# Seven block products for eight in the second gated stage of a fused attention and MLP kernel

## The chip, the cores and the metric

One core of a Trainium2 chip runs the whole program. The metric is the device time of one execution in microseconds (us). The engines are TensorE (PE, with its weight loads shown apart as PEld), VectorE (DVE), ScalarE (ACT), GpSimd (POOL) and SyncE (SP), which here issues nearly all DMAs.

## What is computed

Three parts follow each other on 3072 tokens of 384 features. The last one is the part that the change touches.

```
x1 = leaky_mlp(gated_linear_attention(q, k, v, alpha))   # first part and stage 1: 384 -> 2048 -> 384
a  = x1 @ w1                                             # 384 -> 1024
b  = x1 @ w2                                             # 384 -> 1024
out = ((a * b) @ w3) @ w_out                             # 1024 -> 1024 -> 384
```

All of it is in 32 bits. The kernel folds `w3 @ w_out` into one 1024 x 384 matrix, called w34, so that the last line is one product.

## The kernel before, in words

A product of two 32-bit operands is made of three matmuls: each operand is split into a rounded high part (by an ACT copy) and the rest (by a DVE subtraction), and high by high, high by low and low by high are summed in one PSUM bank (`three`, L418, `mm3`, L413, whose matmuls all carry L416; `split`, L152 to L154). A matmul has 128 rows of contraction, 128 outputs and 512 tokens (384 columns for w34). The tokens are six tiles T of 512.

The attention and stage 1 run interleaved for T = 0 to 5: `G1` makes a block f of the 16 of the hidden layer (nine matmuls, then ACT, DVE, ACT, DVE at L428, L430, L435, L436), and `G2` two blocks later adds its output product (L444 to L447). While the last tile, T = 5, runs in stage 1, the attention is over, and the kernel loads and splits the weights of stage 2 beside it: `load_wo2`, `load_w3`, `load_x1(0)` and `convert_w12` (L532 to L567). The split w1 and w2 blocks take the places of the stage 1 weights `r_in[j]` that have been used: 16 blocks, of which four are started in T = 5 (`TAIL`) and twelve in the next step.

Then w34 is made (L595 to L606): eight times 24 matmuls of 384 columns, called tile `w` in the profile, its results split into `r_out[0..7]` (L600, L601).

Stage 2 (L662 to L679) goes over 6 tiles and 8 blocks j of 128 hidden features. `product` makes the banks of a and b for (T, j), nine matmuls each (three blocks of 128 features times three), tile `ab`; ACT copies a out, DVE multiplies b by it (L624), ACT and DVE split the product (L73, L627; tile `cs`). `project` then makes the output product of the block before, nine matmuls into three banks (tile `acc<-cs`), and after the last block copies the banks out and writes them (L635 to L637). So the matmuls of one block's output product stand behind the next block's input products. `load_x1(T + 1)` reads and splits a tile of x1 (L555 to L557), one tile ahead. `extremes` reads the attention's alpha back in eight pieces and takes its smallest and largest values (L643 to L647); `verdict` (L649 to L660) sets a flag from them that selects a slow repetition after the end if alpha is out of its range, which it is not here.

The order on SP is that of the program. On the other engines instructions are put in order when the kernel is built, by priority and by a model of their times, except where `keep_in_program_order` fixes the order. PSUM has eight banks of 512 columns: `pacc` has six, under the names acc0, acc1 and acc2 with _0 or _1, and `pab` has two. A bank, or an SBUF buffer of a pool, is written again when what read it has ended. `later(k, fn)` runs fn k calls of `tick()` later.

Of the kernel before, what the change touches and what calls it, by code (L numbers as in the profile page):

```python
# [9 lines left out]
F32 = mybir.dt.float32  # L10
# [6 lines left out]
AX = mybir.AxisListType  # L17
# [25 lines left out]
BEHIND = 400  # L43
BLK = 2 * DM
NSP = NJ * (3 * DM + 1024)
TAIL = 4
ALPHA_MIN, ALPHA_MAX = 0.78, 1.28
P_FLOOR = 2.0 ** -60

# [15 lines left out]
def fused_kernel(ctx, tc, qk, al, vv, wf, ws, m_alpha, ident, maskn, out):  # L65
# [90 lines left out]
    def flat(ap):  # L156
        return ap if len(ap.shape) == 2 else ap.rearrange("p a b -> p (a b)")
# [296 lines left out]
    with tc.manual_schedule(engines={mybir.EngineType.SP}):  # L454
# [66 lines left out]
        for g in range(NG + LAG):  # L521
            T, f = seq[g] if g < NG else (NTA, 0)
            if (T, f) == (NTA - 1, 2):
                attn.close()
                late = ExitStack()
                wl = late.enter_context(tc.tile_pool(name="wl", bufs=1))
                w34 = ExitStack()
                wsp = w34.enter_context(tc.tile_pool(name="ws", bufs=1))
                wo2_s = wsp.tile([128, 2, NJ, DM], F32R, name="wo2_s")
                w3_s = []  # L530

                def load_wo2(j):  # L532
                    t = wsp.tile([128, DM], F32, tag="y34", name="wo2", bufs=3)
                    sp.dma_start(out=t, in_=wo2_d[:, j])
                    later(2, lambda: split(wo2_s[:, 0, j], wo2_s[:, 1, j], t, dve))

                def load_w3(i):
                    y = wsp.tile([128, NJ, 128], F32, tag="y34", name="w3y", bufs=3)
                    sp.dma_start(out=flat(y), in_=w3_d[:, i * 1024:(i + 1) * 1024])
                    t = wsp.tile([128, 2, NJ, 128], F32R, tag="w3", name="w3", bufs=2)  # L540
                    for k in range(0, NJ, 4):
                        q = slice(k, k + 4)
                        if i < 2:
                            later(3 + k // 4, lambda q=q: split(t[:, 0, q], t[:, 1, q], y[:, q], dve))
                        else:
                            split(t[:, 0, q], t[:, 1, q], y[:, q], dve)
# [6 lines left out]
                def load_x1(T):  # L553
                    y = wl.tile([128, KD, TA], F32, tag="x1y", name="x1y")
                    sp.dma_start(out=y, in_=x1_d[T])  # L555
                    new_x(T)
                    split(xt[T][:, 0], xt[T][:, 1], y, dve)  # L557

                later(2 * SETTLE, lambda: load_x1(0))
                left = list(range(2 * NJ))  # L560

                def convert_w12():
                    j = left.pop(0)
                    t = r_in[j]
# [30 lines left out]
        for i in range(NJ):  # L595
            t = w3_s[i]
            ps = bank([128, DM], "w34", 0)
            mm3(ps, [m for k in range(NJ) for m in three((t[:, 0, k], t[:, 1, k]), (wo2_s[:, 0, k], wo2_s[:, 1, k]))],
                True, True)
            copy(r_out[i][:, 0], ps)  # L600
            dve.tensor_tensor(out=r_out[i][:, 1], in0=ps, in1=f32(r_out[i][:, 0]), op=ALU.subtract)  # L601
            if i + 2 < NJ:
                load_w3(i + 2)
            while len(left) > (NJ - 1 - i) * (2 * NJ - TAIL) // NJ:
                convert_w12()
            tick()  # L606
        while due:
            tick()
        w34.close()
        load_x1(1)  # L610
        wx = late.enter_context(tc.tile_pool(name="wx", bufs=1))

        def product(j, x):
            ps = []
            for i in range(2):
                w = r_in[2 * j + i]
                p = pab.tile([128, TA], F32, tag="h", name="ab")
                mm3(p, [m for k in range(KD) for m in three((w[:, 0, k], w[:, 1, k]), (x[:, 0, k], x[:, 1, k]))],
                    True, True)
                ps.append(p)  # L620
            a = gp.tile([128, TA], F32, tag="m", name="a", bufs=1)
            copy(a, ps[0])
            c = gp.tile([128, TA], F32, tag="g", name="c")
            dve.tensor_tensor(out=c, in0=ps[1], in1=a, op=ALU.mult)  # L624
            s = gp.tile([128, 2, TA], F32R, tag="gs", name="cs", bufs=3)
# [4 lines left out]
        def project(j, s, accs, dst, op):  # L630
            for m in range(KD):
                c = slice(m * 128, (m + 1) * 128)
                mm3(accs[m], three((r_out[j][:, 0, c], r_out[j][:, 1, c]), (s[:, 0], s[:, 1])), j == 0, j == NJ - 1)
                if j == NJ - 1:
                    o = op.tile([128, TA], F32, tag="x1", name="o", bufs=KD)  # L635
                    copy(o, accs[m])
                    sp.dma_start(out=dst[m * 128:(m + 1) * 128], in_=o)  # L637

        NPART = 2 * B
        ext = wx.tile([128, 2, NPART], F32, name="ext")  # L640
        alv = al.rearrange("b (u c) p a t -> (b u) p c (a t)", u=2)

        def extremes(i):  # L643
            t = wx.tile([128, NC_B // 2, NP * CH], F32, tag="alx", name="alx")
            sp.dma_start(out=t, in_=alv[i])
            later(6, lambda: [dve.tensor_reduce(out=ext[:, a, i:i + 1], in_=t, op=op, axis=AX.XY)
                              for a, op in enumerate((ALU.min, ALU.max))])  # L647

        def verdict():  # L649
# [7 lines left out]
            ps = pab.tile([1, 1], F32, tag="h", name="cnt")  # L657
            for a in range(2):
                pe.matmul(ps, bad[:, a:a + 1], one, start=a == 0, stop=a == 1)
            dve.tensor_copy(flag, ps)  # L660

        prev = None  # L662
        for q in range(NTA * NJ):
            T, j = divmod(q, NJ)
            if j == 0:
                if 1 <= T < NTA - 1:
                    load_x1(T + 1)
                accs = None
            if q % 4 == 2 and q // 4 < NPART:
                extremes(q // 4)  # L670
            if q == 4 * NPART + 10:
                verdict()
            s = product(j, xt[T])
            if prev:
                project(*prev)
            accs = accumulators((T + 1) % 2) if j == 0 else accs
            prev = (j, s, accs, out[:, T * TA:(T + 1) * TA], wx)
            tick()
        project(*prev)  # L679
        assert not due  # L680
    late.close()

# [1 line left out]
    with tc.If(bad > 0):  # L684
# [85 lines left out]
                sp.dma_start(out=x1_d[bass.ds(T, 1)].rearrange("b p k t -> p (b k) t"), in_=x)  # L770

        with tc.tile_pool(name="fx", bufs=2) as fx:
            with tc.For_i(0, NTA, 1) as T:
                y = fx.tile([128, KD, TA], F32, name="x1")
                sp.dma_start(out=y, in_=x1_d[bass.ds(T, 1)].rearrange("b p k t -> p (b k) t"))
# [1 line left out]
                split(e[:, 0], e[:, 1], y, dve)  # L777
                accs = accumulators(0)
                for j in range(NJ):
                    project(j, product(j, e), accs, out[:, bass.ds(T * TA, TA)], gp)  # L780


# [49 lines left out]
```

## Time and profile before

| | |
|---|---|
| Median of 3 runs | 845.78 us (845.17 to 845.91) |
| Profiled execution, first to last instruction | 850.3 us (the page gives this span alone and no time around it) |
| Mean granted TensorE clock | 0.992 of full speed |
| PE busy | 827.5 us, 97% |
| DVE busy | 458.1 us, 54% |
| ACT busy | 355.3 us, 42% |
| HBM read and written | 75.63 MB and 18.35 MB |

The profiled execution is 4.5 us longer than the median. A busy PE is not by itself a PE at its peak, since matmuls overlap; the spacing of matmuls in the chain of waits tells more.

### The profile page before, as it was taken

The page shows a single profiled execution, that of the slowest core. Times are in us where ns is not written, and L with a number is a line of the kernel's source. Part 1 is how long each engine was busy: PE and PEld are TensorE (multiplying, and loading weights), DVE is VectorE, ACT ScalarE, POOL GpSimd, SP SyncE. Part 2 cuts the span into 40 slices and gives each one's busy share as a digit, 9 for nine tenths or more (in the row PEclk, how much of TensorE's full clock was granted, in tenths as well). Part 3 has the DMA queues.
Part 4 walks back from the last instruction along what each step waited for, and adds up shares of the span by engine and source line. Part 5 has one row for each costly group of instructions (what it writes and reads, how often), then busy time and mean ns, then how long its engine had stood idle before and what let it go on. Part 6 is the DMA issues. An engine that isn't in the chain of part 4 may idle for free.

```text
span 850.3 us, 12693 instructions
## 1 busy us (share of the span) xinstructions
PE 827.5 (97%) x5158; PEld 676.9 (80%) x5158; DVE 458.1 (54%) x640; ACT 355.3 (42%) x562; POOL 14.5 (2%) x56
## 2 busy tenths in 40 slices
PE   7889899999999999999999999999999999999996
PEld 4567788888888788878888889988888888888885
DVE  6899966765776477656435634552433435222221
ACT  3567655444554455554435534422223232222222
POOL 1010000000000000000000000000000000000000
PEclk9999999999999999999999999999999999999999
DMA  8557555321654466536003306420302203010101
GB/s 314 180 206 216 181 206 180 99 87 52 217 185 169 149 217 215 166 135 209 33 19 112 124 1 221 142 84 1 127 21 75 75 19 131 1 38 0 38 1 41
DMA packets 49106, 99.60 MB, mean 117 GB/s; under 512 B 4880, under 2 KB 25488, under 8 KB 49040
## 3 DMA queue, kind: packets, MB, share of 16 engines
q1 hardware_dynamic: 48800, 98.62, 34.3%
q8 instruction: 42, 0.69, 0.3%
q14 instruction: 24, 0.20, 0.1%
q10 hardware_dynamic: 240, 0.10, 0.0%
HBM read 75.63 MB, written 18.35 MB: 111 GB/s over the span
## 4 chain that ended last, share of the span: by engine, by line
PE 80%; DVE 7%; DMA 4%; ACT 3%; issue 2%; SPq 1%; DVEq 0%; ACTq 0%
PE ab L416 23%; PE h L416 18%; PE acc L416 12%; PE acc L444 6%; PE acc L445 6%; PE acc L447 6%; PE w L416 4%; DMA al<-in_al_dram 3%; PE uy L247 2%; DMA qk<-in_qk_dram 1%; PE scp L247 1%; DVE y L149 1%; DVE g L430 1%; DVE al L221 1%; DVE sc L282 1%
## 5 line engine op out<-in xcount | busy, mean ns | idle before, releaser
L416 PE MATMUL h<-x,w 128*128 128x512 f32 x864 | 214.7, 393 | 3.9 <-DVE g L430 2.3
L416 PE MATMUL ab<-x,w 128*128 128x512 f32 x864 | 203.7, 389 | 0.0
L416 PEld LDWEIGHTS h<-x,w 128*128 128x128 f32 x864 | 161.4, 188 | 40.3 <-DVE g L430 3.3
L416 PEld LDWEIGHTS ab<-x,w 128*128 128x128 f32 x864 | 162.1, 188 | 33.6
L444 PE MATMUL acc<-gs,w 128*128 128x512 f32 x288 | 115.2, 400 | 0.0
L624 DVE TENSOR_TENSOR c<-ab,a 128x512 f32<-128x512 f32 x48 | 33.1, 690 | 148.3 <-PE ab L416 148.2
L445 PE MATMUL acc<-gs,w 128*128 128x512 f32 x288 | 112.7, 391 | 0.0
L430 DVE SCALAR_TENSOR_TENSOR g<-h,salpha,u 128x512 f32<-128x512 f32 x96 | 71.7, 747 | 72.2 <-ACT u L428 72.2
L416 PE MATMUL acc<-cs,w 128*128 128x512 f32 x432 | 105.8, 389 | 0.0
L428 ACT ACTIVATE u<-h,sgn 128x512 f32<-128x512 f32 x96 | 65.4, 681 | 85.9 <-PE h L416 85.8
L435 ACT ACTIVATE gs<-g,sgn 128x512 fp32r<-128x512 f32 x96 | 69.3, 722 | 72.1 <-DVE g L430 72.0
L436 DVE SCALAR_TENSOR_TENSOR gs<-g,sgn,gs 128x512 fp32r<-128x512 f32 x96 | 71.8, 748 | 42.6 <-ACT gs L435 41.6
L416 PEld LDWEIGHTS acc<-cs,w 128*128 128x128 f32 x432 | 81.0, 188 | 17.2 <-DVE cs L627 0.4
L447 PE MATMUL acc<-gs,w 128*128 128x512 f32 x288 | 80.9, 389 | 0.0
L73 ACT ACTIVATE a<-ab 128x512 f32<-128x512 f32 x48 | 28.7, 597 | 113.5 <-PE ab L416 113.5
L73 ACT ACTIVATE cs<-c 128x512 fp32r<-128x512 f32 x48 | 30.2, 630 | 89.9 <-DVE c L624 89.9
L444 PEld LDWEIGHTS acc<-gs,w 128*128 128x128 f32 x288 | 54.4, 189 | 12.8 <-issue 1.0
L447 PEld LDWEIGHTS acc<-gs,w 128*128 128x128 f32 x288 | 54.1, 188 | 11.5
L445 PEld LDWEIGHTS acc<-gs,w 128*128 128x128 f32 x288 | 54.4, 189 | 10.6
L627 DVE TENSOR_TENSOR cs<-c,cs 128x512 fp32r<-128x512 f32 x48 | 33.2, 691 | 30.8 <-ACT cs L73 30.8
L142 ACT ACTIVATE top<-raw 128x768 f16<-128x768 bf16 (+1 forms) x39 | 41.7, 1069 | 18.0 <-DVE y L149 9.4
L221 DVE TENSOR_TENSOR_SCAN al<-al,scan 128x516 f32<-128x516 f32 x24 | 29.4, 1227 | 24.6 <-DMA al<-in_al_dram 24.6
(73 smaller groups left out, 682.0 us busy)
## 6 DMA issues: line engine op xcount, KB each, us to landing
raw<-in_ws_dram SPq DMA_DIRECT2D x22, 767.8 KB, 5.3
qk<-in_qk_dram SPq DMA_DIRECT2D x24, 512.0 KB, 4.8
raw<-in_wf_dram SPq DMA_DIRECT2D x16, 767.8 KB, 6.0
ws_d<-y SPq DMA_DIRECT2D x22, 384.0 KB, 2.6
al<-in_al_dram SPq DMA_DIRECT2D x24, 256.0 KB, 4.1
v<-in_vv_dram SPq DMA_DIRECT2D x24, 256.0 KB, 4.8
alx<-in_al_dram SPq DMA_DIRECT2D x8, 768.0 KB, 4.5
x_d<-x1e SPq DMA_DIRECT2D x18, 256.0 KB, 4.2
```

The source lines that it names most:

```text
L73: act.activation(out=out, in_=in_, func=AF.Copy)
L142: ins = act.activation(out=z[:, :n].bitcast(F16).rearrange("p (n c) -> p n c", c=2)[:, :, 1], in_=t.bitcast(BF16)[:, :, 2], func=AF.Copy)
L221: scan = dve.tensor_tensor_scan(out=flatP, data0=flatP, data1=scan1.rearrange("p a t -> p (a t)"), initial=0.0, op0=ALU.mult, op1=ALU.max)
L416: pe.matmul(ps, w, x, start=first and i == 0, stop=last and i == n - 1)
L428: both = [act.activation(out=u, in_=ps, func=AF.Identity, scale=sg)]
L430: both += [dve.scalar_tensor_tensor(out=gt, in0=ps, scalar=sa, in1=u, op0=ALU.mult, op1=ALU.max)]
L435: act.activation(out=s[:, 0], in_=gt, func=AF.Identity, scale=sg)
L436: dve.scalar_tensor_tensor(out=s[:, 1], in0=gt, scalar=sg, in1=f32(s[:, 0]), op0=ALU.mult, op1=ALU.subtract)
L444: pe.matmul(acc[T][m], r_out[f][:, 0, c], s[:, 0], start=f == 0, stop=False)
L445: pe.matmul(acc[T][m], r_out[f][:, 1, c], s[:, 0], start=False, stop=False)
L447: pe.matmul(acc[T][m], r_out[f][:, 0, c], s[:, 1], start=False, stop=f == NF - 1)
L627: dve.tensor_tensor(out=s[:, 1], in0=c, in1=f32(s[:, 0]), op=ALU.subtract)
```

## The change

Stage 2 takes two tiles, T and T + 1, at a time. For a block j the input products form a matrix of two rows (w1's and w2's block j) by two columns (the two tiles), summed over three blocks of 128 features, which is twelve block products. Over the first two feature blocks the eight products are replaced by seven (Strassen's method in Winograd's form); the third feature block keeps its four. That is 11 block products for 12, so 33 matmuls for 36 in each `unit` (pair p, block j). The weights' combinations s1 to s4 are made once in `convert_w12`, the tokens' t1 to t4 once for each pair in `x_blocks`. Of the products that share a bank, a later one is added onto what ACT or DVE has read out between (`first=False`).

The order of all matmuls of stage 2 is fixed as written (`pinned`). The output product of the pair's first tile runs two blocks behind (`behind`, `LAG` = 2); that of the second tile (`cs2`, eight buffers) runs behind the pair, 24 matmuls for each of three banks (`fin`). The last group of a unit (`rest`, called `tail`) is put into the next unit. w34 goes to `r_out[8..15]`, since `r_out[0..7]` hold weight combinations. Alpha's extremes are taken in 24 pieces for eight, and the verdict moves to the last pair's end. The diff, cut to its core:

```diff
+    w34 = r_out[NJ:]
...
                 def load_w3(i):
-                    y = wsp.tile([128, NJ, 128], F32, tag="y34", name="w3y", bufs=3)
+                    for k in range(0, NJ, 4):
+                        y = wsp.tile([128, 4, 128], F32, tag="y34", name="w3y", bufs=4)
...
                 def convert_w12():
                     j = left.pop(0)
-                    y = wsp.tile([128, DM], F32, tag="w12", name="w12", bufs=3)
-                    sp.dma_start(out=y, in_=w12_d[:, j])
-                    split(flat(t[:, 0]), flat(t[:, 1]), y, dve)
+                    y = wsp.tile([128, 2, KD, 128], F32, tag="w12", name="w12", bufs=2)
+                    sp.dma_start(out=y, in_=w12_d[:, 2 * j:2 * j + 2].rearrange("p i (k c) -> p i k c", k=KD))
+                    (a11, a12, a13), (a21, a22, _) = ([y[:, i, k] for k in range(KD)] for i in range(2))
+                    split(r_in[2 * j][:, 0], r_in[2 * j][:, 1], y[:, 0], dve)
+                    for to, x0, x1, op in ((a13, a11, a21, ALU.subtract), (a21, a21, a22, ALU.add),
+                                           (a11, a21, a11, ALU.subtract), (a12, a12, a11, ALU.subtract)):
+                        dve.tensor_tensor(out=to, in0=x0, in1=x1, op=op)
+                    split(r_in[2 * j + 1][:, 0], r_in[2 * j + 1][:, 1], y[:, 1], dve)
+                    split(r_out[j][:, 0], r_out[j][:, 1], flat(y[:, 0]), dve)
+                def x_blocks(p, part):
...
+                    if part == 0:
+                        b = [read(2 * p, 0), read(2 * p + 1, 0), read(2 * p, 1)]
...
+                        keep("b11", b[0])
+                        minus(b[0], b[1], b[0])
+                        keep("t1", b[0])
+                        keep("b21", b[2])
+                        xb["raw"] = b + [read(2 * p + 1, 1)]
+                        return
...
+                    minus(t1, b22, t1)
+                    keep("t2", t1)
+                    keep("b22", b22)
+                    minus(b21, b21, t1)
+                    minus(b12, b22, b12)
+                    b31, b32 = read(2 * p, 2), read(2 * p + 1, 2)
+                    keep("b31", b31)
+                    keep("b32", b32)
+                    keep("t3", b12)
+                    keep("t4", b21)
...
-            if T == NTA - 1 and f >= NF - TAIL:
+            if T == NTA - 1 and f % 2 == 1 and f > 1:
                 later(2, convert_w12)
...
+        def unit(j, tail, behind):
...
+            u, y = (pacc.tile([128, TA], F32, tag=f"acc{i}_{j % 2}", name="uy"[i]) for i in range(2))
+            go(u, ("a11", "b11"))
+            copy(c1, u)
+            go(y, ("a12", "b21"), ("a13", "b31"))
+            dve.tensor_tensor(out=c1, in0=y, in1=c1, op=ALU.add)
+            tail()
+            z = pacc.tile([128, TA], F32, tag="acc2_0", name="z")
+            go(z, ("s1", "t1"))
+            copy(p5, z)
+            behind(0)
+            behind(1)
+            go(u, ("s2", "t2"), first=False)
+            copy(c2, u)
+            go(z, ("s4", "b22"), ("a13", "b32"), first=False)
+            dve.tensor_tensor(out=c2, in0=z, in1=c2, op=ALU.add)
+            go(y, ("a23", "b32"))
+            behind(2)
+            go(u, ("s3", "t3"), first=False)
+            dve.tensor_tensor(out=b2, in0=u, in1=p5, op=ALU.add)
+            dve.tensor_tensor(out=b2, in0=y, in1=b2, op=ALU.add)
+            dve.tensor_tensor(out=c2, in0=c2, in1=b2, op=ALU.mult)
+            second = split_c(c2, "cs2", NJ)
+            def rest():
+                go(u, ("a22", "t4"), ("a23", "b31"), first=False)
+                dve.tensor_tensor(out=c1, in0=u, in1=c1, op=ALU.mult)
+                first.append(split_c(c1, "cs1", 3))
...
+            for j in range(NJ):
+                extremes(q)
+                behind = (lambda m, j=j: add_out(j - LAG, m, cs1[j - LAG][0], accs[m])) if j >= LAG else nothing
+                tail, a, b = unit(j, tail, behind)
...
+            for j in range(NJ - LAG, NJ):
+                if j == NJ - 1:
+                    tail()
+                for m in range(KD):
+                    add_out(j, m, cs1[j][0], accs[m]) if j < NJ - 1 else None
+            if p + 1 < NTA // 2:
+                x_blocks(p + 1, 0)
+            fin = [pacc.tile([128, TA], F32, tag=f"acc{m}_0", name="o2") for m in range(2)]
+            for m in range(KD):
+                if m == 1:
+                    for i in range(KD):
+                        add_out(NJ - 1, i, cs1[NJ - 1][0], accs[i])
+                        emit(T, i, accs[i])
+                    if p + 1 < NTA // 2:
+                        x_blocks(p + 1, 1)
+                    else:
+                        verdict()
+                if m == 2:
+                    fin.append(pacc.tile([128, TA], F32, tag="acc2_1", name="o2"))
+                for j in range(NJ):
+                    add_out(j, m, cs2[j], fin[m])
+                emit(T + 1, m, fin[m])
```

`keep` is a `split` of one block, `read` one DMA of a 128 x 512 block of x1 into one of four buffers, and `emit` a copy and a DMA of one output bank through three buffers. `x_blocks(0, 0)` is set off in T = 5 and `x_blocks(0, 1)` in the first step of w34. The slow repetition behind the end is adapted to the new places of the weights and does not run.

## Rows read from the trace of the kernel before

**Rows 1.** The page, busy time of each engine over the span.
```profile
PE 827.5 (97%) x5158; PEld 676.9 (80%) x5158; DVE 458.1 (54%) x640; ACT 355.3 (42%) x562; POOL 14.5 (2%) x56
```

**Rows 2.** Busy time by stretch: T = 5 of stage 1, w34, stage 2.
```profile
core 0: us, PE busy (x) PEld busy (x) DVE busy (x) ACT busy (x) POOL busy (x), PEclk, DMA share, GB/s
451.20:515.73 64.53, 64.53 (x286) 53.46 (x285) 32.67 (x48) 31.73 (x51) 0.00 (x0) 1.00 0.23 78
515.73:549.03 33.30, 33.30 (x193) 33.30 (x193) 18.65 (x32) 17.83 (x35) 0.00 (x0) 1.00 0.63 213
549.03:843.54 294.51, 294.50 (x1301) 242.88 (x1299) 100.56 (x123) 73.49 (x118) 0.00 (x0) 1.00 0.13 46
```

**Rows 3.** The chain in order of time through stage 2: start us, us, what.
```profile
549.03 8.20 PE ab L416 x36
557.24 2.04 PE acc L416 x9
559.27 4.08 PE ab L416 x18
...
839.15 4.39 PE acc L416 x18
```

**Rows 4.** Groups by line and shape from 515.7 us on: busy us, mean ns.
```profile
L416 PE MATMUL ab<-x,w 128*128 128x512 f32 x864 | 203.7, 389 | 0.0
L416 PE MATMUL acc<-cs,w 128*128 128x512 f32 x432 | 105.8, 389 | 0.0
L627 DVE TENSOR_TENSOR cs<-c,cs 128x512 fp32r<-128x512 f32 x48 | 33.2, 691 | 30.8 <-ACT cs L73 30.8
L73 ACT ACTIVATE cs<-c 128x512 fp32r<-128x512 f32 x48 | 30.2, 630 | 89.9 <-DVE c L624 89.9
L73 ACT ACTIVATE a<-ab 128x512 f32<-128x512 f32 x48 | 28.7, 597 | 113.5 <-PE ab L416 113.5
L646 DVE TENSOR_REDUCE ext<-alx 128x1 f32<-128x1536 f32 x16 | 27.5, 1747 | 9.1 <-DMA alx<-in_al_dram 9.1
L154 DVE TENSOR_TENSOR x<-x1y,x 128x1536 fp32r<-128x1536 f32 x5 | 8.8, 1758 | 3.7 <-ACT x L73 3.7
L154 DVE TENSOR_TENSOR w<-w,w 128x384 fp32r<-128x384 f32 x12 | 6.4, 555 | 4.7 <-ACT w L73 4.7
```

**Rows 5.** Timeline where w34 ends and stage 2 begins.
```profile
549.07 0.49 ACT L73 ACTIVATE w<-w 128x384 fp32r<-128x384 f32 x1 [3.67 <-PE w L416]
549.59 0.56 DVE L601 TENSOR_TENSOR w<-w,w 128x384 fp32r<-128x384 f32 x1 [0.43 <-ACT w L73]
551.15 0.60 ACT L73 ACTIVATE a<-ab 128x512 f32<-128x512 f32 x1 [1.59 <-PE ab L416]
```

**Rows 6.** Timeline of the end.
```profile
840.65 0.69 DVE L627 TENSOR_TENSOR cs<-c,cs 128x512 fp32r<-128x512 f32 x1 [0.70 <-ACT cs L73]
841.40 1.70 PEld L416 LDWEIGHTS acc<-cs,w 128*128 128x128 f32 x8 [0.40 <-DVE cs L627]
842.80 2.32 SPq L637 DMA_DIRECT2D out_dram<-o  x3
```

**Rows 7.** Timeline of DVE in T = 5, one late `g` and the next.
```profile
473.97 1.76 DVE L154 TENSOR_TENSOR x<-x1y,x 128x1536 fp32r<-128x1536 f32 x1 [0.80 <-ACT x L73]
475.65 0.74 DVE L430 SCALAR_TENSOR_TENSOR g<-h,salpha,u 128x512 f32<-128x512 f32 x1
...
478.17 0.74 DVE L430 SCALAR_TENSOR_TENSOR g<-h,salpha,u 128x512 f32<-128x512 f32 x1
```

**Rows 8.** DMA issues: KB each, median us from issue to landing.
```profile
al<-in_al_dram SPq DMA_DIRECT2D x24, 256.0 KB, 4.1
...
x1y<-x_d SPq DMA_DIRECT2D x6, 768.0 KB, 5.9
out_dram<-o SPq DMA_DIRECT2D x18, 256.0 KB, 2.1
```

**Rows 9.** Timeline of PE at two waits in earlier stages.
```profile
293.62 0.74 PE L247 MATMUL uy<-v,kT 128*64 128x64 f32 x16 [1.98 <-ACT x1e L73]
...
375.20 0.69 PE L247 MATMUL uy<-v,kT 128*64 128x64 f32 x16 [0.95 <-ACT x1e L73]
```

**Rows 10.** Stretches around these two waits; the column behind POOL is the granted clock.
```profile
292.00:294.00 2.00, 0.38 (x12) 0.39 (x14) 0.40 (x1) 1.97 (x5) 0.00 (x0) 1.00 0.00 0
294.00:296.00 2.00, 2.00 (x29) 1.67 (x24) 0.00 (x0) 0.54 (x2) 0.00 (x0) 0.53 0.03 8
296.00:298.00 2.00, 2.00 (x50) 2.00 (x48) 0.78 (x2) 0.82 (x3) 0.00 (x0) 0.62 0.00 0
...
375.00:377.00 2.00, 1.80 (x44) 1.63 (x48) 0.00 (x0) 1.12 (x3) 0.00 (x0) 1.00 0.00 0
```

More of the change, by code (lines that the diff above doesn't have):

```diff
@@ L45 @@
 NSP = NJ * (3 * DM + 1024)
-TAIL = 4
 ALPHA_MIN, ALPHA_MAX = 0.78, 1.28
@@ L525, in fused_kernel @@
                 late = ExitStack()
-                wl = late.enter_context(tc.tile_pool(name="wl", bufs=1))
-                w34 = ExitStack()
-                wsp = w34.enter_context(tc.tile_pool(name="ws", bufs=1))
+                wl = late.enter_context(tc.tile_pool(name="wl", bufs=4))
+                w34p = ExitStack()
+                wsp = w34p.enter_context(tc.tile_pool(name="ws", bufs=1))
                 wo2_s = wsp.tile([128, 2, NJ, DM], F32R, name="wo2_s")
@@ L552, in fused_kernel @@
                     later(NJ + 1 + 2 * i, lambda i=i: load_w3(i))
[L553 to L560, printed above, removed]
+                left = list(range(NJ))
                 def convert_w12():
                     j = left.pop(0)
[L564 to L567 removed]
+                    y = wsp.tile([128, 2, KD, 128], F32, tag="w12", name="w12", bufs=2)
[7 more added lines that the diff above has]
+                    split(r_out[j][:, 0], r_out[j][:, 1], flat(y[:, 0]), dve)
@@ new lines, in x_blocks, with read, keep, minus @@
+                def x_blocks(p, part):
+                    def read(T, k):
+                        y = wl.tile([128, TA], F32, tag="x1y", name="x1y")
+                        sp.dma_start(out=y, in_=x1_d[T][:, k])
+                        return y
+                    def keep(name, y):
+                        t = xb[name]
+                        split(t[:, 0], t[:, 1], y, dve)
+                    def minus(to, x0, x1):
+                        dve.tensor_tensor(out=to, in0=x0, in1=x1, op=ALU.subtract)
+                    if part == 0:
+                        b = [read(2 * p, 0), read(2 * p + 1, 0), read(2 * p, 1)]
+                        t = xp.tile([128, 2, KD, TA], F32R, tag="x", name="xb0")
+                        for i, name in enumerate(("b11", "b21", "t1")):
+                            xb[name] = t[:, :, i]
+                        keep("b11", b[0])
[4 more added lines that the diff above has]
+                        return
+                    t1, b12, b21, b22 = xb.pop("raw")
+                    t = xp.tile([128, 2, KD, TA], F32R, tag="x", name="xb1")
+                    for i, name in enumerate(("t2", "b22", "b32")):
+                        xb[name] = t[:, :, i]
+                    for name in ("b31", "t3", "t4"):
+                        xb[name] = gp.tile([128, 2, TA], F32R, tag="gs", name="xb2", bufs=3)
+                    minus(t1, b22, t1)
[8 more added lines that the diff above has]
+                    keep("t4", b21)
@@ L569, in fused_kernel @@
+                xb = {}
+                later(2 * SETTLE, lambda: x_blocks(0, 0))
             if g in spans:
@@ L599, in fused_kernel @@
                 True, True)
-            copy(r_out[i][:, 0], ps)
-            dve.tensor_tensor(out=r_out[i][:, 1], in0=ps, in1=f32(r_out[i][:, 0]), op=ALU.subtract)
+            copy(w34[i][:, 0], ps)
+            dve.tensor_tensor(out=w34[i][:, 1], in0=ps, in1=f32(w34[i][:, 0]), op=ALU.subtract)
             if i + 2 < NJ:
                 load_w3(i + 2)
-            while len(left) > (NJ - 1 - i) * (2 * NJ - TAIL) // NJ:
+            if left:
                 convert_w12()
+            if i == 0:
+                x_blocks(0, 1)
             tick()
@@ L608, in fused_kernel, with pinned, duo, blocks_of @@
             tick()
-        w34.close()
-        load_x1(1)
+        w34p.close()
         wx = late.enter_context(tc.tile_pool(name="wx", bufs=1))
[L613 to L625, printed above, removed]
+        def pinned(ps, pairs, first=True, last=True):
+            n = len(pairs)
+            for i, (w, x) in enumerate(pairs):
+                tc.keep_in_program_order(pe.matmul(ps, w, x, start=first and i == 0, stop=last and i == n - 1,
+                                                   skip_group_check=True))
+        def duo(t, k):
+            return t[:, 0, k], t[:, 1, k]
+        def blocks_of(j):
+            r3 = r_out[j].rearrange("p h (k c) -> p h k c", k=KD)
+            names = ("a11", "a12", "a13", "s1", "a22", "a23", "s2", "s4", "s3")
+            tiles = [r_in[2 * j]] * KD + [r_in[2 * j + 1]] * KD + [r3] * KD
+            return {n: duo(t, i % KD) for i, (n, t) in enumerate(zip(names, tiles))}
+        def split_c(c, tag, bufs):
+            s = wx.tile([128, 2, TA], F32R, tag=tag, name=tag, bufs=bufs)
             copy(s[:, 0], c)
@@ L628, in product, with add_out, emit @@
             return s
[L630 to L639, printed above, removed]
+        def add_out(j, m, s, ps):
+            c = slice(m * 128, (m + 1) * 128)
+            pinned(ps, three((w34[j][:, 0, c], w34[j][:, 1, c]), (s[:, 0], s[:, 1])), j == 0, j == NJ - 1)
+        def emit(T, m, ps):
+            o = gp.tile([128, TA], F32, tag="x1", name="o", bufs=KD)
+            copy(o, ps)
+            sp.dma_start(out=out[m * 128:(m + 1) * 128, T * TA:(T + 1) * TA], in_=o)
+        NPART = NSTEP
         ext = wx.tile([128, 2, NPART], F32, name="ext")
-        alv = al.rearrange("b (u c) p a t -> (b u) p c (a t)", u=2)
         def extremes(i):
-            t = wx.tile([128, NC_B // 2, NP * CH], F32, tag="alx", name="alx")
-            sp.dma_start(out=t, in_=alv[i])
-            later(6, lambda: [dve.tensor_reduce(out=ext[:, a, i:i + 1], in_=t, op=op, axis=AX.XY)
+            t = wx.tile([128, NP, CH], F32, tag="alx", name="alx")
+            sp.dma_start(out=t, in_=al[i // NC_B, i % NC_B])
+            later(1, lambda: [dve.tensor_reduce(out=ext[:, a, i:i + 1], in_=t, op=op, axis=AX.XY)
                               for a, op in enumerate((ALU.min, ALU.max))])
@@ L656, in verdict @@
                 dve.tensor_scalar(out=bad[:, a:a + 1], in0=m[:, a:a + 1], scalar1=lim, scalar2=None, op0=cmp)
-            ps = pab.tile([1, 1], F32, tag="h", name="cnt")
+            ps = pacc.tile([1, 1], F32, tag="acc1_1", name="cnt")
             for a in range(2):
-                pe.matmul(ps, bad[:, a:a + 1], one, start=a == 0, stop=a == 1)
+                tc.keep_in_program_order(pe.matmul(ps, bad[:, a:a + 1], one, start=a == 0, stop=a == 1))
             dve.tensor_copy(flag, ps)
-        prev = None
@@ L663, in fused_kernel @@
[L663 to L677, printed above, removed]
-            tick()
@@ new lines, in fused_kernel @@
+        nothing = lambda *_: None
+        for p in range(NTA // 2):
+            T = 2 * p
+            tail = nothing
+            cs1, cs2 = [], []
+            accs = [pacc.tile([128, TA], F32, tag="acc2_1", name="o0")]
+            accs += [pab.tile([128, TA], F32, tag="h", name="o1") for _ in range(2)]
+            for j in range(NJ):
+                q = p * NJ + j
+                extremes(q)
+                behind = (lambda m, j=j: add_out(j - LAG, m, cs1[j - LAG][0], accs[m])) if j >= LAG else nothing
+                tail, a, b = unit(j, tail, behind)
+                cs1.append(a)
+                cs2.append(b)
+                tick()
+            for j in range(NJ - LAG, NJ):
[5 more added lines that the diff above has]
+                x_blocks(p + 1, 0)
+            tick()
+            fin = [pacc.tile([128, TA], F32, tag=f"acc{m}_0", name="o2") for m in range(2)]
[13 more added lines that the diff above has]
+                emit(T + 1, m, fin[m])
+            tick()
@@ L772, in fused_kernel, with product, project @@
         with tc.tile_pool(name="fx", bufs=2) as fx:
+            for j in range(NJ):
+                t = r_in[2 * j + 1]
+                y = fx.tile([128, DM], F32, name="w2y")
+                sp.dma_start(out=y, in_=w12_d[:, 2 * j + 1])
+                split(flat(t[:, 0]), flat(t[:, 1]), y, dve)
+            def product(j, x):
+                ps = []
+                for i in range(2):
+                    w = r_in[2 * j + i]
+                    p = pab.tile([128, TA], F32, tag="h", name="ab")
+                    mm3(p, [m for k in range(KD) for m in three((w[:, 0, k], w[:, 1, k]), (x[:, 0, k], x[:, 1, k]))],
+                        True, True)
+                    ps.append(p)
+                a = gp.tile([128, TA], F32, tag="m", name="a", bufs=1)
+                copy(a, ps[0])
+                c = gp.tile([128, TA], F32, tag="g", name="c")
+                dve.tensor_tensor(out=c, in0=ps[1], in1=a, op=ALU.mult)
+                s = gp.tile([128, 2, TA], F32R, tag="gs", name="cs", bufs=3)
+                copy(s[:, 0], c)
+                dve.tensor_tensor(out=s[:, 1], in0=c, in1=f32(s[:, 0]), op=ALU.subtract)
+                return s
+            def project(j, s, accs, dst):
+                for m in range(KD):
+                    c = slice(m * 128, (m + 1) * 128)
+                    mm3(accs[m], three((w34[j][:, 0, c], w34[j][:, 1, c]), (s[:, 0], s[:, 1])), j == 0, j == NJ - 1)
+                    if j == NJ - 1:
+                        o = gp.tile([128, TA], F32, tag="x1", name="o", bufs=KD)
+                        copy(o, accs[m])
+                        sp.dma_start(out=dst[m * 128:(m + 1) * 128], in_=o)
             with tc.For_i(0, NTA, 1) as T:
@@ L779, in fused_kernel @@
                 for j in range(NJ):
-                    project(j, product(j, e), accs, out[:, bass.ds(T * TA, TA)], gp)
+                    project(j, product(j, e), accs, out[:, bass.ds(T * TA, TA)])
 def kernel(**inputs):
```

19 lines of the change are left out of this document (14 added, 5 removed).

## The prediction

> **What bounds the kernel now.** I read the page first: PE is busy for 97% of the span, DVE for half, ACT for less [rows 1]. An average over stages says little, so the stretches come next: in T = 5 of stage 1, in w34 and in stage 2 PE is busy without a gap, at full granted clock, while DVE is busy 51%, 56% and 34% of the time [rows 2]. Since a busy PE need not be at its pace, the chain comes third. In stage 2 it is PE alone: 36 matmuls in 8.20 us, 9 in 2.04, 18 in 4.08, and so on to the end [rows 3]. Each is 0.2267 us per matmul (8.16 / 36, 2.04 / 9), whether nine follow each other into one bank (ab) or three banks take three each (acc). The 864 + 432 = 1296 matmuls [rows 4] would take 293.8 us at that pace; the stretch is 294.5 [rows 2]. So 0.7 us of stage 2 is waiting, and only fewer matmuls can shorten it.
>
> **The sum** is taken as differences in the profiled execution (span 850.3 us, the only time its page gives) and applied to the median of the runs, 845.78; stage 2 runs at one steady pace there, so I carry the differences over unscaled. 0.2%, or 1.7 us, is about what a measurement of this kernel can tell from no change.
>
> *Removed.* In each of 3 x 8 units 33 input matmuls stand for 36. That is 72 matmuls, 72 x 0.2267 = **-16.3 us**. The output products stay 432. Only a twelfth of the input products goes, since the third feature block keeps its four. The pace itself has no reason to change: the operands' shapes stay, and three matmuls to a bank cost what nine do [rows 3].
>
> TensorE: Matmul & The Clock Gate, section Back-to-back issue gap, in the Trainium skill, gives about 131 ns for a matmul of 512 columns in a real stream; by that the term would be -9.4 us. The trace has 227 ns, and the trace decides.
>
> *The end.* Today's last output product waits for its own split: the DVE subtraction ends at 841.34, the weight load starts at 841.40 [rows 6], and the last 18 matmuls take 4.39 us where 18 others take 4.08 [rows 3]. After the change 24 matmuls into one bank stand last, with operands long ready: **-0.3**. One output bank is copied and written at the end, for three; their issue takes 2.32 us [rows 6]. As I cannot see what of that delays the end, the gain lies between 0 and 1.5, an estimate from two thirds of it; I take 0. The verdict's four tiny matmuls move and cost the same.
>
> *The bank of y in the first unit.* Waits come where a bank is rewritten. An evacuation takes: 0.08 us from the last matmul to ACT (ab began at 549.03, nine matmuls end at 551.07, the copy starts at 551.15), 0.60 us of copy [rows 5], 0.06 us back to the weight load [rows 6], in all 0.74. The eighth w34 block uses acc1_0, which the first unit's y wants three matmuls after w34 has ended, 549.03 + 0.68 = 549.71. That bank is still read by ACT and then DVE until 550.15 [rows 5]. With 0.06 back and a weight load ahead of the matmul (0.2, an estimate from the two starts of 841.40 and the 0.3 lost there) the wait is **+0.7**.
>
> *The bank of z.* `p5` is copied from z and z is added to afterwards. From block 2 on nine matmuls lie between (2.04 us), which covers 0.74. In blocks 0 and 1 of each pair nothing is behind yet, so only three do (0.68 us). The wait is at least 0.06; with the weight load behind it 0.3; with a split's copy (0.63, [rows 4]) ahead of it on ACT 0.9. Six times, so 0.4 to 5.4; I take 0.3 each, as only block 1 has a split to do at that moment: **+1.8**. The other reuses have cover: u after `c1` 21 matmuls (9 in block 0), u after `c2` at least 9, the tail's u 9 (2.04 us against 0.08 + 0.69 + 0.06 for the `b2` addition), the output operands one unit or more.
>
> *Between pairs (twice).* 13 DVE operations of 0.69 us and nine ACT copies of 0.63 [rows 4] replace the splits of whole tiles (1.76 on DVE). The first part has the 24 matmuls of the first `fin` and more ahead. The second part is the long one: on SP the reads of b31 and b32 are queued behind the output DMAs of the pair, and they need buffers that t1 and b22 leave. From the end of `add_out(7)`: about 3.5 us for t2, b22 and t4's difference, 4.1 for a 256 KB read (as alpha's; 768 KB of x1 took 5.9, an output write 2.1 [rows 8]), 1.4 for the split, so 9 us. The cover is 48 `fin` matmuls and six of the unit, 54 x 0.2267 = 12.2 us. So 3 us remain, and a bad order on ACT (three output buffers for four copies in a row, each held until its DMA has landed) could use them up. Bounds 0 to 3 each; **+0.6** for both, near the lower end because the durations that I know fit.
>
> *Weights.* A conversion is now three splits of 384 columns and four 128-column operations: on DVE 3 x 0.555 + 4 x 0.29 (from the line through 0.555 and 0.691 [rows 4]) = 2.8 us, eight times, seven of them set off in T = 5. There DVE rises from 32.7 us to 32.7 + 19.7 + 2.8 (first part of x_blocks) - 4.0 (four old splits and x1's) = 51 of 64.5 us; in w34 it stays near 19 of 33 (18.65 - 12 x 0.555 - 1.76 + 2.8 + 9 x 0.69). It goes at nothing, because stage 1 has slack in this place: one `g` came 1.94 us late behind the 1.76 us split (475.65 for 473.71, at 4.08 us a block) and the next 0.4 [rows 7], and PE lost nothing [rows 2]. Without that cover a late conversion costs its 2.8 us less 2; bounds 0 to 3.
>
> *DVE and ACT in stage 2.* A unit needs eight DVE operations of 0.69 and two reductions (512 columns for 1536, about 0.6 each by [rows 4]): 6.7 us, and five copies on ACT, 3.1 us, in 42 matmuls or 9.5 us. Neither is the bound; alpha's 24 small reads have 9.5 us each.
>
> Sum: -16.3 - 0.3 + 0.7 + 1.8 + 0.6 = -13.5, so **832.3 us**. With all waits at their least and the end's gain: -17.0, or 828.8. With z, the pairs and the weights at their most: 845.8 - 16.6 + 0.7 + 5.4 + 6 + 3 = 844.3, which needs all of them at once.
>
> **Rivals.**
> *A, the pairs' border shows.* The chain of b31 is 4 to 6 us longer than reckoned, and PE stands for 2 us or so twice. This has a second price: where PE had stood 1.98 us [rows 9], after two microseconds in which it was busy only 0.38, the granted clock of the next two stretches was 0.53 and 0.62 [rows 10], almost its lower level (1.2 GHz for 2.4); that lost about 0.47 x 2 + 0.38 x 2 = 1.7 us. A stop of 0.95 us kept the clock [rows 9, 10]. So 2 x (2 + 1.7) = 7.4 more: 839.7. For it: SP's order and the one set of buffers. Against it: 3 us of slack.
>
> *B, slower: each unit waits for a bank.* u takes four groups in turn and each must be read before the next is added. If DVE stands at alpha's reductions, their read not landed, when u's `b2` addition is due, the tail waits for u, 24 times. Free are 2.04 - 0.83 = 1.2 us; past that every 0.56 us of delay in each unit (13.5 / 24) eats the gain. A read that lands 2.2 us late costs 1.0 a unit: 832.3 + 24 = 856. For it: alpha's buffer is single, so a read cannot start before the last unit's reductions. Against it: it has a whole unit, 9.5 us, for 4.1 [rows 8], and other covers are 2 us for 0.74.
> Perfetto Trace Analysis, section Matmuls under Optimizing Tensor Performance, in the Trainium skill, speaks for this rival: independent groups should rotate through different banks so that the reading of one lies beside the next. Here other banks' groups stand between, which by the durations in the rows is enough from block 2 on.
>
> *C, nothing gained.* The matmuls go but PE is held elsewhere to the same total, by z's six waits, both borders and late conversions at their upper ends: 844.3; it needs all of these, which have separate causes, and so gets little chance. That PE's pace depends on something that the change breaks also belongs here; the even 0.2267 us in both patterns [rows 3] speaks against it.
>
> **How the numbers follow.** The forecast, with its own range of 829 to 835, has 0.70; A, 835 to 842, 0.21; C 0.03; B and the like 0.06. The range 828.8 to 838.5 holds the forecast and more than half of A, some 0.8. Faster: 0.70 + 0.21 = 0.91; within 0.2%: 0.03; slower: 0.06.
>
> **What would show it.** Right: 792 input matmuls for 864, at 0.227 us; PE's waits near 0.7 us at the first y and some tenths at z in blocks 0 and 1; none at `tail`. Stage 2 then lasts about 281 us. A shows as one gap on PE at the start of the second and third pair, released by a split of b31, and a dip of the clock. B shows as the same gap in every unit, released by DVE. Gaps in T = 5 released by `g` would show the weights' term wrong. Wrong altogether: a pace off 0.227, or a stage 2 above 290 us.

## The result, and the profile after

The changed kernel takes **838.1 us** (median of 4, 836.48 to 840.13) against 845.85 beside it; the ratio is 0.9898, 95% interval 0.9872 to 0.9924, so 6.4 to 10.8 us less. The forecast was 832.3 in a range of 828.8 to 838.5: the time fell and lies in the range, 0.4 us below its top; the gain was put too high.

First the page's busy time, which answers to [rows 1]:

```profile
PE 812.8 (97%) x5086; PEld 659.6 (79%) x5086; DVE 544.4 (65%) x841; ACT 378.5 (45%) x615; POOL 13.9 (2%) x56
```

72 matmuls fewer, DVE with 841 instructions for 640. Then the stretches, T = 5, w34 and stage 2, which answer to [rows 2]:

```profile
core 0: us, PE busy (x) PEld busy (x) DVE busy (x) ACT busy (x) POOL busy (x), PEclk, DMA share, GB/s
449.00:513.56 64.56, 64.56 (x286) 53.28 (x285) 49.87 (x101) 40.22 (x72) 0.00 (x0) 1.00 0.36 112
513.56:547.90 34.34, 33.59 (x194) 33.27 (x193) 16.12 (x30) 14.56 (x29) 0.00 (x0) 1.00 0.42 142
547.90:832.05 284.15, 283.62 (x1228) 228.91 (x1227) 171.79 (x273) 91.40 (x156) 0.00 (x0) 1.00 0.16 50
```

T = 5 has not changed, though DVE is busy 49.9 us of it for 32.7. w34 is 1.0 us longer. Stage 2 is 10.4 us shorter, where the forecast had 13.5. The clock is at its upper level throughout. Next who waited, from T = 5 to the end (engine and line, for whom, us in total, times, longest):

```profile
PE w L416 <- ACT w L72: 0.7, 1, 0.7
PE y L659 <- DVE w L643: 0.5, 1, 0.5
```

Two waits with 1.2 us are all that this view has, and stage 2 is 6.7 us above 1224 x 0.2267 = 277.5. The chain in order of time shows where the rest is; it answers to [rows 3]:

```profile
549.07 1.66 PE y L659 x6
...
552.10 1.65 PE z L659 x6
554.44 1.36 PE u L659 x6
...
559.90 1.65 PE z L659 x6
...
567.01 1.40 PE o L659 x6
...
620.64 2.10 PE o L659 x9
...
624.12 18.90 PE o L659 x81
```

Six matmuls should take 1.36 us, as u's do. z's six in blocks 0 and 1 take 0.29 more: waits that the list above leaves out, and that stand in the groups below at z's weight load, released by ACT's copy p. And the output products, tile o, are slow without any wait: six in 1.40, nine in 2.10, 81 in 18.90, which is 233.3 ns each. The groups that answer to [rows 4] show it as a longer mean for o than for y, and the DVE prices (the profile leaves numbers in names out: p is `p5`, b is `b2`, cs is `cs1` or `cs2`):

```profile
L659 PE MATMUL o<-cs,w 128*128 128x512 f32 x432 | 107.8, 395 | 0.0
L659 PE MATMUL u<-xb,w 128*128 128x512 f32 x360 | 94.4, 390 | 0.0
...
L659 PE MATMUL z<-xb,w 128*128 128x512 f32 x216 | 57.7, 393 | 0.1
L659 PE MATMUL y<-xb,w 128*128 128x512 f32 x216 | 57.0, 390 | 0.5 <-DVE w L643 0.5
...
L659 PEld LDWEIGHTS z<-xb,w 128*128 128x128 f32 x216 | 40.1, 188 | 11.1 <-ACT p L72 2.6
...
L692 DVE TENSOR_REDUCE ext<-alx 128x1 f32<-128x512 f32 x48 | 32.2, 679 | 6.7 <-DMA alx<-in_al_dram 6.6
...
L737 DVE TENSOR_TENSOR b<-u,p 128x512 f32<-128x512 f32 x24 | 16.6, 691 | 21.5 <-PE u L659 21.2
```

Summed from the starts of neighbouring matmuls, what is above 226.7 ns in stage 2 is: 3.0 us in spacings that begin with an o matmul, 0.6 in the u matmuls behind them, 1.7 at the six z, 0.8 at the first y, and 0.4 for the verdict, as before. That is 6.5 of the 6.7.

So the questions are: why o is slow; whether the waits are what they seem; and whether the matmul count alone is the gain.

### The profile page after: what moved, and what is told of

Its sections match the earlier page's. It is cut to its first block, busy times and chain, and to the rows that moved or that the text cites. A ratio compares the mean times of both kernels' runs of the same rounds, so it can differ in the third digit from the quotient of the medians.

```text
span 838.4 us, 12828 instructions
## 1 busy us (share of the span) xinstructions
PE 812.8 (97%) x5086; PEld 659.6 (79%) x5086; DVE 544.4 (65%) x841; ACT 378.5 (45%) x615; POOL 13.9 (2%) x56
## 4 chain that ended last, share of the span: by engine, by line
PE 77%; DVE 8%; DMA 7%; ACT 3%; issue 2%; SPq 1%; DVEq 0%; ACTq 0%
PE h L416 18%; PE o L659 12%; PE u L659 10%; PE z L659 6%; PE y L659 6%; PE acc L444 6%; PE acc L447 6%; PE acc L445 6%; DMA al<-in_al_dram 4%; PE w L416 4%; PE uy L247 2%; DVE al L221 2%; DVE y L149 1%; PE scp L247 1%; DMA x<-yT 1%
## 5 line engine op out<-in xcount | busy, mean ns | idle before, releaser
L659 PE MATMUL o<-cs,w 128*128 128x512 f32 x432 | 107.8, 395 | 0.0
L659 PEld LDWEIGHTS o<-cs,w 128*128 128x128 f32 x432 | 81.0, 188 | 19.1
L659 PE MATMUL u<-xb,w 128*128 128x512 f32 x360 | 94.4, 390 | 0.0
L659 PEld LDWEIGHTS u<-xb,w 128*128 128x128 f32 x360 | 67.5, 188 | 14.9
L72 ACT ACTIVATE c<-u 128x512 f32<-128x512 f32 x48 | 28.7, 598 | 86.4 <-DVE b L737 53.0
L659 PE MATMUL z<-xb,w 128*128 128x512 f32 x216 | 57.7, 393 | 0.1
L659 PE MATMUL y<-xb,w 128*128 128x512 f32 x216 | 57.0, 390 | 0.5 <-DVE w L643 0.5
L659 PEld LDWEIGHTS z<-xb,w 128*128 128x128 f32 x216 | 40.1, 188 | 11.1 <-ACT p L72 2.6
L659 PEld LDWEIGHTS y<-xb,w 128*128 128x128 f32 x216 | 40.5, 188 | 9.4 <-DVE w L643 0.9
```

Of the source, the lines that this page charges most:

```text
L72: act.activation(out=out, in_=in_, func=AF.Copy)
L659: tc.keep_in_program_order(pe.matmul(ps, w, x, start=first and i == 0, stop=last and i == n - 1, skip_group_check=True))
```

## Experiments

**Why the output products are slow.** Each pair of weight load and matmul reads two operands from SBUF: the weights (128 columns) and the moving operand (512 columns). By the layout of the program, all moving operands of stage 1, w34 and stage 2 in the kernel before start 96 bytes past a multiple of 128 in a partition of SBUF, and so do the weights. In the changed kernel cs1 and cs2 lie behind a tile of 192 bytes (`ext`) and start at 32. Theory: the address. Rival: 24 matmuls in a row into one bank, or the order.

```diff
-        ext = wx.tile([128, 2, NPART], F32, name="ext")
+        ext = wx.tile([128, 2, 32], F32, name="ext")[:, :, :NPART]
```

> The small tile ahead of cs1 and cs2 takes 256 bytes for 192, so both start 96 bytes past a multiple of 128 like every other moving operand; no instruction is changed. Address theory: the 432 output matmuls go at 227 ns for 233, stage 2 is shorter by 432 x 6.6 ns = 2.9 us, and the time falls by as much. Structure theory: no change of the pace nor of the time.

Measured: 832.73 us (830.97 to 835.16), ratio 0.9849, interval 0.9823 to 0.9874, against 846.75 for the kernel before. The chain of this kernel at the places shown above (start, us, what):

```profile
614.92 2.04 PE o L659 x9
...
618.32 18.36 PE o L659 x81
```

and its stage 2, in the columns of the stretches above:

```profile
542.80:823.26 280.46, 279.93 (x1229) 229.06 (x1227) 171.65 (x273) 91.35 (x156) 0.00 (x0) 1.00 0.16 50
```

18.36 for 18.90, and stage 2 is 3.7 us shorter: the 3.0 of the o matmuls, the 0.6 behind them. No instruction was changed, so place is the cause and structure is not. (c1, c2 and alpha's buffer lie behind `ext` too and moved with it; TensorE does not read them.)

**Which place.** Eight buffers at eight offsets (`split_at` is `split_c` with a start k inside a larger buffer; c2 gets one buffer for two):

```diff
...
-            second = split_c(c2, "cs2", NJ)
+            second = split_at(c2, (24, 28, 0, 4, 8, 12, 16, 20)[j])
```

> The eight cs2 buffers are set 16 bytes apart, at 0, 16, 32, 48, 64, 80, 96 and 112 bytes past a multiple of 128 (c2 has one buffer for two, to make room). Address theory (the product w34 x cs is slow, 233 ns for 227, because its moving operand starts 32 bytes past a multiple of 128, where all other moving operands start at 96): within one bank's 24 matmuls the spacing changes every three matmuls, with 227 at offset 96 and 233 at 32, and other values at the other offsets. Structure theory (24 matmuls in a row into one bank, or operands written by the same split as in the units): 233 ns at every offset.

Measured: 835.77 us, one run. From the starts of the matmuls in the trace, 18 spacings for each buffer (17 for one):

```
bytes of cs2 past the weights, modulo 128:   0     16     32     48     64     80     96    112
mean spacing within the buffer, ns:        226.3  233.2  231.0  232.5  228.1  232.1  229.9  233.7
```

(The theory's offset 96 is distance 0 here, since the weights lie at 96.) The spacing changes with the buffer, so the structure theory falls again. Only one of the eight keeps the full pace. Offset 32, distance 64, should have shown 233 by the theory and shows 228, so the single values are not constants; three matmuls to a buffer may be too few for a pace to settle. Counted modulo 256 the spread is no simpler: such a buffer takes 4224 bytes, 33 x 128, so every second one lies 128 further, and the eight distances become 0, 144, 32, 176, 192, 80, 224 and 112. The one at 192 shows 228.1, and 192 is where cs1 and cs2 lie in the changed kernel, at 233.3 throughout. So its own distance does not settle the spacing of a buffer whose neighbours lie elsewhere.

> The kernel before, with a 64-byte tile at the front of SBUF, so that all its buffers behind it start 32 bytes past a multiple of 128 for 96, weights and moving operands alike; no other instruction than one small memset is added. If the place of the moving operand alone sets the pace, the 3024 matmuls of 512 columns take 6.6 ns more each, 20 us, and stage 2 lasts 303 us for 294.5. If it is the moving operand's place against the weights', or only the structure of the output products, nothing changes: 845 to 848 us.

The edit is a tile at the front of SBUF, with one memset:

```diff
+    gap = const.tile([128, 16], F32, name="gap")
     idn = const.tile([128, 128], F32, name="idn")
...
+        dve.memset(gap, 0.0)
```

Measured: 847.72 us (845.6 to 850.46), ratio 1.0016, interval 1.0001 to 1.0031; stage 2 takes 294.5 us (546.21 to 840.69) as before. Its chain begins:

```profile
546.21 8.20 PE ab L417 x36
554.41 2.04 PE acc L417 x9
```

With weights and moving operands both at 32 nothing is slow. So the offset alone is not it; the distance between the two is. The reverse, only the moving operands shifted:

```diff
+    gapp = ctx.enter_context(tc.tile_pool(name="gapp", bufs=1))
+    gap = gapp.tile([128, 16], F32, name="gap")
     xp = ctx.enter_context(tc.tile_pool(name="xp", bufs=2))
...
+        dve.memset(gap, 0.0)
```

> The kernel before, with a 64-byte tile between the weights and the moving operands of both stages: weights stay 96 bytes past a multiple of 128, the moving operands x, gs and cs go to 32. If the distance between the two modulo 128 sets the pace, the matmuls of 512 columns of stage 1 and 2 go at 233 ns for 227: stage 2 lasts 294.5 + 1296 x 0.0066 = 303.1 us, and the whole is up to 3024 x 0.0066 = 20 us slower, about 865 us. If the slow pace needs the order of the output products of the changed kernel as well, it stays at 846 us.

Measured: 851.39 us (850.63 to 852.62), ratio 1.0046, interval 1.0031 to 1.0061: slower, by 3.6 us and not by 20. The chain and stage 2 of this kernel:

```profile
553.85 2.06 PE acc L418 x9
555.91 4.12 PE ab L418 x18
```

```profile
545.60:842.90 297.30, 297.27 (x1301) 243.11 (x1299) 100.68 (x123) 73.51 (x118) 0.00 (x0) 1.00 0.13 46
```

229 ns for 227, everywhere in stage 2, and in stage 1 too (229 by the starts of its matmuls). The distance counts here too, but a distance of +64 bytes costs 2.2 ns a matmul where cs1 and cs2, which lie at 192 modulo 256 from their weights (-64), cost 6.6. My size for this run was wrong because I had taken the distance modulo 128, by which +64 and -64 are one. That 0 keeps the full pace holds in every kernel here that has it; the rule for the others stays open.

**Are the waits what they seem?** Three edits, each with its own gap in the trace:

```diff
-            u, y = (pacc.tile([128, TA], F32, tag=f"acc{i}_{j % 2}", name="uy"[i]) for i in range(2))
+            u, y = (pacc.tile([128, TA], F32, tag=f"acc{i}_{(j + 1) % 2}", name="uy"[i]) for i in range(2))
...
+            if j < LAG:
+                go(y, ("a23", "b32"))
             go(z, ("s4", "b22"), ("a13", "b32"), first=False)
...
-            if i == 0:
+            if i == 3:
                 x_blocks(0, 1)
```

(`fin` and the verdict's bank change places with the units' banks, and the old `go(y, ...)` stays for the later blocks.)

> Three waits are taken out of the changed kernel: in blocks 0 and 1 of a pair y's second product stands ahead of z's (six matmuls behind p5's copy for three); the units begin with the banks that w34 did not use; the second part of the first x_blocks is set off at the fourth w34 block for the first. If these waits are what they look like: six gaps at z of 0.28 us (1.7), the gap at the first y (0.85 with its run-up) and the gap within w34 (0.9) go, and stage 2 and w34 are shorter by 3.4 us together, and so the time. Rival (each wait only hides the next: DVE or ACT are late anyway): the gaps come back at the next user of b2, c2 or b31, and less than 1 us is won.

Measured: 831.86 us (831.82 to 832.1), ratio 0.9829, interval 0.9808 to 0.9849. Its w34 and stage 2:

```profile
509.27:542.58 33.31, 33.31 (x194) 33.31 (x193) 16.30 (x30) 14.79 (x29) 0.00 (x0) 1.00 0.45 146
542.58:824.13 281.55, 281.55 (x1228) 229.43 (x1227) 171.33 (x273) 91.39 (x156) 0.00 (x0) 1.00 0.15 50
```

and one z of its chain:

```profile
546.70 1.36 PE z L659 x6
```

w34 loses its 1.0 us, stage 2 loses 2.6, together 3.6 for 3.4 expected; z's six take 1.36, and PE has no gap in either stretch. Nothing came back elsewhere.

**Both, and the matmul count.** The two edits above in one kernel:

> Both edits together: cs1 and cs2 at the same distance past a multiple of 128 as the weights, and the three waits removed. If the two causes are separate they add: stage 2 lasts 284.1 - 3.7 - 2.6 = 277.8 us, which is 1224 x 0.2267 = 277.5 and the verdict's 0.4, and w34 33.3 for 34.3; against the changed kernel 7.3 us less, about 830 us. If one hides the other, stage 2 stays at 280 or above.

Measured: **829.01 us** (828.14 to 830.63) against 847.77, ratio 0.9783, interval 0.9765 to 0.9801. This beats both kernels; it is 6.6 us under the changed kernel's 835.58 beside it, for 7.3 expected. Its w34 and stage 2:

```profile
510.13:543.43 33.30, 33.30 (x193) 33.30 (x193) 16.34 (x30) 14.59 (x29) 0.00 (x0) 1.00 0.44 146
543.43:821.30 277.87, 277.87 (x1228) 229.47 (x1227) 170.96 (x273) 91.25 (x156) 0.00 (x0) 1.00 0.16 51
```

277.9 us is 1224 matmuls at 0.2267 and the verdict: at this pace nothing is left to remove there but matmuls. The two causes add: 3.7 and 2.6 apart, 6.3 together.

And one product made twice:

```diff
             go(u, ("a11", "b11"))
+            go(u, ("a11", "b11"))
```

> As the kernel with both edits, but the first product of each unit (a11 by b11) is made twice into the same bank, the second time from the start again, so that a unit has 36 input matmuls as before the change. If the gain is the matmul count alone: stage 2 grows by 72 x 0.2267 = 16.3 us to 294.2, which is the 294.5 of the kernel before, and the time is that of the kernel before within its spread. If something else in the new order had helped or hurt, the two stretches differ by more than 1 us.

Measured: 846.13 us (844.29 to 847.1), ratio 0.9982, interval 0.997 to 0.9994. Stage 2 of this kernel:

```profile
545.10:839.30 294.20, 294.20 (x1301) 243.04 (x1299) 172.76 (x273) 90.94 (x156) 0.00 (x0) 1.00 0.15 48
```

With 36 input matmuls in a unit again the stretch is 294.2 for 294.5 before [rows 2]. All that seven products for eight give here is the 72 matmuls; DVE's 72 us of further work in stage 2 cost nothing, as this kernel does it too. Of the median's 1.6 us, 0.3 lies in stage 2 and 0.8 behind the last matmul (6.0 us for 6.8), by the profiles.

**What comes before w34.** The changed kernel once more, beside the last two kernels and the one with only the moving operands shifted:

> The changed kernel once more, unaltered, beside the others on one chip. Stage 2 lasted 284.1 us and w34 34.3 in its profile; both stretches should come out the same to 0.3 us. What lies ahead of w34 began w34 at 513.4 us in one profile and at 507.9 to 509.7 in three kernels with the same work there: if that part only varies from execution to execution, w34 begins anywhere from 508 to 516 here, and the median lies between 835 and 840 us; if the changed kernel is really slower there, w34 begins above 511 again.

Measured: 835.58 us (833.98 to 838.67), ratio 0.987, interval 0.9848 to 0.9893. w34 takes 34.3 and stage 2 284.1, to a tenth as in the first profile:

```profile
507.60:541.94 34.34, 33.59 (x193) 33.27 (x193) 16.09 (x30) 14.55 (x29) 0.00 (x0) 1.00 0.41 142
541.94:826.08 284.14, 283.61 (x1229) 228.98 (x1227) 171.94 (x273) 91.42 (x156) 0.00 (x0) 1.00 0.16 50
```

But w34 begins at 507.4 us, just under the 508 to 516 expected, where it began at 513.4 in the other profile of the same kernel. Over the ten profiles of this study it begins between 507.4 and 515.6 us, with TensorE's order ahead of it the same in the two kernels. Most of the 6.0 us between the two profiles of the changed kernel are waits of PE for DVE's g, which the list of waits of the first has with 4.5 us:

```profile
PE h L416 <- DVE g L430: 4.5, 2, 3.4
```

They stand at 97 us (3.4) and 264 us (1.1), long before the changed part; the list of the second profile has none for g ahead of w34. Why DVE was late there stays open. The spread is as large as the gain, so stretches of two profiles tell these kernels apart better than medians of a few runs.

## Why the prediction was right, and where it was off

From w34 to the end of the profiled execution (w34, stage 2, what lies behind the last matmul): before 33.30 + 294.51 + 6.76, after 34.34 + 284.15 + 6.35. That is **-9.7 us where the sum said -13.5**, inside both intervals (6.4 to 10.8, and 9.1 to 12.9 in the second comparison). The medians of the first comparison differ by 7.8 us. The other 2 us are inside its interval; ahead of w34 single profiles spread over 8 us, so they may lie there, but no run shows it.

The range held by its width. 838.1 lies in the band that the prediction gave to rival A, 835 to 842, and A did not happen; and the sum was missed by a term that was not in it.

- *The matmuls, -16.3.* Right: 72 fewer, and putting as many back made 294.2 of 277.9, 16.3 us or 227 ns each. TensorE: Matmul & The Clock Gate, section Back-to-back issue gap, in the Trainium skill, gives about 131 ns for 512 columns in a real stream; no two matmuls of 512 columns start less than 215 ns apart in the trace of the changed kernel.
- *The pace.* **The step that failed**: "The pace itself has no reason to change: the operands' shapes stay". The shapes stayed, the places did not. The output products went at 233.3 ns, which with the matmuls behind them cost 3.6 us, against a miss of 3.8; beside it w34's +1.0 is nearly cancelled by the pairs' 0.6 that did not come and 0.4 gained at the tail. By the prediction's own sign ("Wrong altogether: a pace off 0.227") the 432 output matmuls were wrong and the 792 input matmuls right. I could not have read it from the trace of before, in which one pace rules, but I had taken the pace for a property of shapes and banks without asking what else moves with the new buffers.
- *z's six waits, +1.8.* 1.7. *The first y, +0.7.* 0.8. Both were sums of durations from rows, and both went when the bank or the order was changed: the mechanism was right, too. Perfetto Trace Analysis, section Matmuls under Optimizing Tensor Performance, in the Trainium skill, asks that independent groups rotate through banks; the trace agrees where only three matmuls lie between two uses of z (0.28 us each time), and with nine between, or six in the run with the order changed, it shows no cost.
- *Weights, at nothing with bounds 0 to 3.* T = 5 lost nothing with DVE busy 49.9 of 64.6 us (51 forecast). w34 lost 1.0, a wait that the sum had at nothing, though DVE was busy only 16 of its 34 us. A stretch's mean did not show it; the order did, in the timeline of w34 of the changed kernel:

```profile
521.37 1.15 ACT L72 ACTIVATE xb<-x1y 128x512 fp32r<-128x512 f32 x2 [0.21 <-DMA x1y<-x_d]
...
522.87 1.14 ACT L72 ACTIVATE xb<-x1y 128x512 fp32r<-128x512 f32 x2
...
526.49 1.14 ACT L72 ACTIVATE w<-w3y 128x512 fp32r<-128x512 f32 x2
526.54 1.28 DVE L154 TENSOR_TENSOR w<-w3y,w 128x512 fp32r<-128x512 f32 x2
527.16 20.73 PE L416 MATMUL w<-wo_s,w 128*128 128x384 f32 x118 [0.75 <-ACT w L72]
```

  The blocks of x1, not wanted before 548, are split ahead of a w3 block that PE wants at 526.4. With these blocks set off three steps later the loss was gone.
- *Between pairs, +0.6, and rival A.* No gap at either border and no dip of the clock. The border's timeline:

```profile
629.76 2.00 ACT L72 ACTIVATE o<-o 128x512 f32<-128x512 f32 x3 [4.24 <-PE o L659]
...
632.55 0.60 ACT L72 ACTIVATE o<-o 128x512 f32<-128x512 f32 x1 [0.79 <-DMA out_dram<-o]
633.61 0.86 SPq L570 DMA_DIRECT2D x1y<-x_d  x2
636.78 2.19 ACT L72 ACTIVATE xb<-x1y 128x512 fp32r<-128x512 f32 x4 [3.63 <-DMA x1y<-x_d]
637.45 2.50 DVE L154 TENSOR_TENSOR xb<-x1y,xb 128x512 fp32r<-128x512 f32 x4 [10.79 <-ACT xb L72]
```

  The fourth output copy waits for a buffer, as feared (0.79), and the reads stand behind it on SP; but t2, b22 and all differences had been made by 625.5 us, ahead of these copies, and the read took 3.2 us from issue to the first copy. All blocks are ready at 639.95; the next pair begins at 643.0. The 3 us of slack were 3.
- *Rival B* did not come: no gap at a tail in any unit. *Rival C* did not come as a whole, since the time fell; but its last part, that PE's pace depends on something that the change breaks, is what happened to the output products. The even 0.2267 us in both patterns [rows 3], which spoke against it, could not show this, as both patterns had their operands at the same distance from the weights.
- *The end, -0.3 and 0 to -1.5.* The wait went; the tail behind the last matmul is 0.4 shorter.

## What to carry to other kernels

PE ran without a gap here, and the saving of 72 matmuls came through in full; part of it was lost again to new waits and to a new pace. Price each new wait from rows first: three of them here were each worth a reordered line. When a change gives an operand a new buffer, compare the spacing of the matmuls that read it with the others: a pace can change with no wait to be seen, and the list of waits does not show it. A stretch whose engines are half idle can still hold up PE, if work that is due later is put ahead of work that is due now.

## What the hardware showed that was not expected

The spacing of a stream of weight load and matmul pairs (512 columns, operands of type fp32r, in which the split halves are stored) depended on where in SBUF the moving operand lies against the weights: 226.7 ns at a distance of 0 modulo 256 bytes, 228.9 at 64, 233.4 at 192, and 228 to 234 at the seven distances that were tried in groups of three, 192 among them at 228. What sets the other values is open. With both shifted by 64 bytes it was 226.7 again. A tile of 192 bytes for one of 256, holding nothing that TensorE reads, cost 3.7 us of stage 2.
